# Spatial gating's rests: the last product of each half on 64 rows instead of 128, the two halves on different rows of TensorE

## The chip, the cores and the metric

The kernel runs on one core of one Trainium2 chip. The metric is the device time of one execution in microseconds, from three runs: their median is 718.81 us, the lowest 718.46, the highest 719.28. A profiled execution of the same kernel lies beside them.

## The reference, cut to what matters

Three layers in a row: a linear attention, a gated convolution layer, and a gated MLP whose second half is mixed over the tokens. The change is in the last one. With 8 batches, 576 tokens, width 512:

```
h = gelu(x @ w_in)                       # 1024 wide
u, v = h[..., :512], h[..., 512:]
v_n = (v - mean(v)) / sqrt(var(v) + 1e-6) * g_ln
v_s = einsum('ts,bsd->btd', w_sg, v_n) + b_sg[None, :, None]
out = x + (u * v_s) @ w_out
```

The line with `einsum` is the one that matters: for each batch a 576x576 matrix is multiplied with the 576x512 matrix of normalised `v`, so it sums over tokens.

## The kernel before, in words

Every large product is made with fp32r operands that are split in a high and a low part: `x*w` becomes `xh*wh + xl*wh + xh*wl`, three TensorE products that add into one PSUM bank. The 576 tokens of a batch are four tiles of 128 tokens and a rest of 64. The rests of several batches are handled together in other products.

The first 321 us do attention and the convolution layer; then comes a loop over the 8 batches that does the MLP. For each batch there are four values of `m` (128 columns of the width each). For one `m` TensorE makes `hu` (12 products of 512 columns), then `sg` for `c = 0` and `c = 1`, the two halves of 288 output tokens. After the four `m` come 48 products `hv` of the next batch and 48 products `out`, each of 512 columns.

One `sg` half (L685 to L697) is 14 products of 288 columns into one bank: three for each of the four token tiles (`v` high with weight high `sgw`, `v` low with `sgw`, `v` high with weight low `sgl`), and two for the 64 rests. The rests of two batches, one even and one odd, sit in the two halves of the 128 partitions. `Rests.hv` (L648) makes from them one operand for each batch, `r[i]`: its own 64 partitions hold the high part, the other 64 the low part. So the first rest product, with `sgw[:, NK]` (the 64 rest weights' high part, twice, one below the other), gives two of the three terms at once. The second rest product gives the third term, high part by low weights. It runs on all 128 rows too: its weight operand, one for even and one for odd batches, `sgw[:, NK + 1 + b % 2]`, holds the low weights in the one half and zeros in the other. `rest_weight` (L523) makes these once.

After the last product of a half VectorE scales the bank into `vs` (L697); after both halves `gated` (L699) multiplies with `u` on VectorE (L707), rounds to the high part on ScalarE (L708), and takes the low part on VectorE (L712), into `gg`, which sits in buffer `Z`. `wout2` (L717) reads it.

In the trace the names are those of reused buffers: `sg<-WV,X` is a rest product (`X` is `X32`, the rests' operand; `WV` holds `sgw`, `G` holds `sgl`, and `X0h`, `X0l`, `Q`, `K`, `V` hold the token tiles or the weights of `out`). The order on each engine is set by a scheduler that the tile framework runs at build time. There are 8 PSUM banks that take turns. The kernel's first part has one other place where TensorE is used in parts: `kv` (L337) makes for each head a 64x64 product, two heads in the two halves of the array's columns (forms `128*64` in the trace: 128 rows, 64 columns).

Of the kernel before, what the change touches and what calls it, by code (L numbers as in the profile page):

```python
# [10 lines left out]
F32R = mybir.dt.float32r  # L11
AF = mybir.ActivationFunctionType
ALU = mybir.AluOpType
# [6 lines left out]
P = 128  # L20
# [12 lines left out]
WC = 256  # L33

LINE = 128
ROOM = {"st": 128, "bst": 32, "bmv": 32, "gcol": 32, "gln": 32, "mhalf": 96, "eps": 32, "cw": 64, "T": S, "X32": 19 * 128}
APART = 8

ORDER = """
# [20 lines left out]
class Slots:  # L60
# [5 lines left out]
    def later(self, slots, fn, rank=1):  # L66

        self.waiting.append((self.now + slots, rank, fn))
# [14 lines left out]
def body(ctx, tc, qT, k, v, gcol, w_val, conv_w, w_out, w_in, g_ln, w_sgT, b_sg, w_out2, out, out_r):  # L83
# [8 lines left out]
    def sb(tag, shape, dtype=F32, bufs=1, o=0):  # L92
        count[0] += 1
        words = math.prod(shape)
        t = pool.tile([P, o + words], dtype, tag=tag, name=f"{tag}_{count[0]}", bufs=bufs,
                      padded_shape=[P, ROOM.get(tag) or -(-(o + words) // LINE) * LINE])[:, o:]
        if len(shape) == 1:
            return t
        d = [f"d{i}" for i in range(len(shape))]
        return t.rearrange(f"p ({' '.join(d)}) -> p {' '.join(d)}", **dict(zip(d, shape)))  # L100

    def tmp(n):

        return sb("T", [S], bufs=7)[:, :n]
# [11 lines left out]
    def f32(x):  # L116
        return x.bitcast(F32)
# [404 lines left out]

    def rest_weight():  # L523
        sgw = p2["sgw"]
        rwh, rwl = sgw[:, NK], [sgw[:, NK + 1], sgw[:, NK + 2]]
        raw = tmp(S)
        for i in range(2):
            dma(raw[i * DH:(i + 1) * DH], w_sgT[4 * P:, :])
        act(rwh, raw, AF.Copy)
        for i in range(2):  # L530
            a = slice(i * DH, (i + 1) * DH)
            z = slice((1 - i) * DH, (2 - i) * DH)
            tt(rwl[i][a], raw[a], f32(rwh[a]), op=ALU.subtract)
            tt(rwl[i][z], raw[z], raw[z], op=ALU.subtract)

    def sg_weight(stage):
        p2["sgw"] = sb("WV", [NK + 3, S], F32R)
        p2["sgl"] = sb("G", [NK, S], F32R)
        for t in range(NK):
            def parts(t=t):  # L540
                act(p2["sgw"][:, t], stage[:, t], AF.Copy)
                tt(p2["sgl"][:, t], stage[:, t], f32(p2["sgw"][:, t]), op=ALU.subtract)

            parts()
# [94 lines left out]
    class Rests:  # L639
# [6 lines left out]
            self.pr = pr  # L646

        def hv(self):  # L648
            r = [p2["r"][:, self.pr % 2, i] for i in range(2)]

            def parts(g):
                for i in range(2):
                    a = slice(i * DH, (i + 1) * DH)
                    o = slice((1 - i) * DH, (2 - i) * DH)
                    act(r[i][a], g[a], AF.Copy)
                    tt(r[i][o], g[a], f32(r[i][a]), op=ALU.subtract)

            hv(*self.y, parts)
            return r

    class Group:

# [19 lines left out]
            gemm3(ps, (p2["wiu"][:, 0], p2["wiu"][:, 1]), m, self.y[:, 0], self.y[:, 1])  # L682
            gelu2(ps, self.u[:, m])

    def sg(b, c, m, vt, rem, vs):  # L685
        ps = bank("sg", CH)
        sl = slice(c * CH, (c + 1) * CH)
        msl = slice(m * P, (m + 1) * P)
        sgw, sgl = p2["sgw"], p2["sgl"]
        mm = []  # L690
        for t in range(4):
            h, l = vt[t]
            mm += [(h, sgw[:, t, sl]), (l, sgw[:, t, sl]), (h, sgl[:, t, sl])]
        mm += [(rem, sgw[:, NK, sl]), (rem, sgw[:, NK + 1 + b % 2, sl])]
        for n, (a, w) in enumerate(mm):
            nc.tensor.matmul(ps, lhsT=a[:, msl], rhs=w, start=(n == 0), stop=(n == len(mm) - 1))  # L696
        later(0, lambda: stt(vs[:, sl], ps, gln_s[:, m:m + 1], p2["bsg"][:, sl], op0=ALU.mult, op1=ALU.add))  # L697

    def gated(b, m, vs, u, ur, gg, ggr):  # L699

# [196 lines left out]
    for b in range(1, B):  # L897
        moe = moes[b] if b == 1 else Moe(atts[b].xh, atts[b].xl, gate, y_main[b])
        nxt = atts[b + 1] if b + 1 < B else None
        nn = atts[b + 2] if b + 2 < B else None  # L900
        group = b % RG == RG - 1
        if b == 2:
            p2["wiv"], p2["wiu"] = (sb(n, [2, NK, D], F32R) for n in ("wiv", "wiu"))
            wi = split_weight(p2["wiv"], w_in, D, D) + split_weight(p2["wiu"], w_in, 0, D)
            behind(loaded, wi[0][0])
            behind(loaded, wi[1][0])
            wi_n = 0
        if b == 1:
            whole = unbroken(lambda: (nn.kv(0), nn.kv(1)))
        for s in range(4 if b == 1 else 0, 8):  # L910
            with tc.issue_after(whole) if whole else ExitStack():
                if s < 4:
                    moe.val(s)
                else:
                    moe.out(s - 4)
            whole = None
            if nxt and s < 3:
                nxt.o(s + 2)
            if nn and s == 3 and not group:
                whole = unbroken(lambda: (nn.kv(0), nn.kv(1)))  # L920
            if nn and s == 3:
                nn.load_q()
            if b + 3 < B and s == 5 and not group:
                atts.append(Attention(b + 3))
                atts[-1].load_kv()
            if nn and s in (6, 7) and not group:
                nn.o(s - 6)
            if nxt and s in ((4, 5) if b == 1 else (5, 7)):
                later(0, lambda a=nxt, m=2 * (s > 4) if b == 1 else s - 5: a.gates((m, m + 1)), 2)
            if s == 2:  # L930
                later(0, atts[b].rest_parts, 2)
            if (b, s) == (B - 3, 7):
                w2 = w2_pieces()
                wi += w2[:4]
            if s in {2: (1, 4, 7), 3: odd, 4: odd, 5: odd, 6: odd, 7: (0,)}.get(b, ()):
                later(0, lambda w=wi[wi_n][1], m=marks[-3]: behind(m, w), 3)
                if wi_n + 2 < len(wi):
                    later(0, wi[wi_n + 2][0], 4)
                wi_n += 1
            if b == B - 1:  # L940
                if s == 0:
                    v_alloc()
                if s == 4:
                    stage = sb("X32", [NK, S])
                    dma(stage, w_sgT[:4 * P, :].rearrange("(t p) s -> p t s", p=P))
                    toks = Tokens(0)
                    toks.load(0)
                if s > 4:
                    toks.load(s - 4)
                    later(0, lambda t=s - 5: toks.split(t), 1)  # L950
            tick()
            marks.append(latest())
        if group:
            moe = Moe(rest["x"][:, 0], rest["x"][:, 1], rest["g"], y_rest[b // RG])
            for s in range(8):
                with tc.issue_after(whole) if whole else ExitStack():
                    if s < 4:
                        moe.val(s)
                    else:
                        moe.out(s - 4)  # L960
                whole = None
                if nn and s == 1:
                    whole = unbroken(lambda: (nn.kv(0), nn.kv(1)))
                if b + 3 < B and s == 2:
                    atts.append(Attention(b + 3))
                    atts[-1].load_kv()
                if nn and s == 3:
                    nn.o(0)
                    nn.o(1)
                if b == B - 1:  # L970
                    if s == 0:
                        toks.split(3)
                    if s < 4:
                        toks.hv(s)
                    if s == 2:
                        rem = Rests(0)
                        later(1, rem.split, 1)
                    if s == 4:
                        sg_weight(stage)
                        rest_weight()  # L980
                        p2["r"] = sb("X32", [2, 2, D], F32R)
                    if s == 5:
                        y_r = Group.load(0)
                    if s == 6:
                        background(w2[4:], 2, 2)
                if b == B - 1 or s % 2:
                    tick()
# [6 lines left out]
    for b in range(B):  # L994
# [9 lines left out]
        for m in range(NK):  # L1004
            u = toks.hu(m)
            tick()
            vs = tmp(S)
            for c in range(2):
                sg(b, c, m, toks.v, rem[b % 2], vs)
                if c:  # L1010
                    gated(b, m, vs, u, grp.u, gg, ggr)
                tick()
            if more and m == 2:
                ntoks = Tokens(b + 1)
                ntoks.load(0)
                ntoks.load(1)
# [78 lines left out]
```

## Time and profile before

| what | value |
|---|---|
| median of 3 runs | 718.81 us (718.46 to 719.28) |
| the profiled execution's own time | 718.38 us |
| its span, first to last instruction | 716.6 us |
| TensorE (PE) busy | 708.3 us, 99% |
| VectorE (DVE) busy | 572.5 us, 80% |
| ScalarE (ACT) busy | 365.4 us, 51% |
| GpSimd (POOL) busy | 160.7 us, 22% |
| granted TensorE clock | full in all 40 slices |

Busy time is the union of an engine's instructions. A matmul's duration in the trace is longer than the step from its start to the next one's start, since matmuls overlap in the array; steps between starts are what adds up to the span. Start times are given in us from the span's start with two digits, durations in line views in ns.

### The profile page before, as it was taken

What the parts mean: (1) busy time and instruction counts of PE and PEld (TensorE: products, weight loads), DVE (VectorE), ACT (ScalarE), POOL (GpSimd) and SP (SyncE); (2) the same over time, 40 slices, a digit from 0 to 9 for tenths busy, and PEclk for the clock granted to TensorE, in tenths of its full rate; (3) what the DMA queues carried; (4) which work ended last, traced back from release to release, by engine and by line L of the source; (5) the groups of instructions that cost most, each with busy time, mean ns of one, the idle gap of its engine ahead of it and who ended that gap; (6) DMA issues with size and microseconds to landing.
All of it is one profiled execution on the core that took longest, in us unless ns stands there. A gap on an engine that the chain in (4) does not pass through costs nothing.

```text
span 716.6 us, 11759 instructions
## 1 busy us (share of the span) xinstructions
PE 708.3 (99%) x4462; PEld 619.6 (86%) x4462; DVE 572.5 (80%) x1111; ACT 365.4 (51%) x747; POOL 160.7 (22%) x180
## 2 busy tenths in 40 slices
PE   8999999999999999999999999999999999999998
PEld 8788888889888888899889888898899898898897
DVE  3999897999899999799867877857867767868662
ACT  2999966575666574664524434335334334335220
POOL 1558435434635532121000000100100100100000
PEclk9999999999999999999999999999999999999999
DMA  9994066227442113541231221122241122111302
GB/s 309 324 301 155 37 222 219 90 102 252 157 168 96 75 53 132 179 136 43 75 118 30 75 89 52 51 74 82 80 147 37 67 75 74 59 59 46 102 1 89
DMA packets 57241, 81.20 MB, mean 113 GB/s; under 512 B 3680, under 2 KB 30304, under 8 KB 56160
## 3 DMA queue, kind: packets, MB, share of 16 engines
q1 hardware_dynamic: 57184, 80.45, 33.5%
q8 instruction: 35, 0.57, 0.3%
q14 instruction: 22, 0.18, 0.1%
HBM read 61.56 MB, written 18.87 MB: 112 GB/s over the span
## 4 chain that ended last, share of the span: by engine, by line
PE 82%; DVE 12%; DMA 2%; ACT 1%; issue 1%; POOL 1%; SPq 0%; DVEq 0%; POOLq 0%
PE sg L696 17%; PE hv L587 14%; PE out L266 14%; PE hu L266 12%; PE y L266 11%; PE val L266 8%; DVE G L457 6%; PE o L358 2%; PE hur L266 2%; PE xT L394 1%; PE kv L337 1%; DVE st L368 1%; DMA V<-in_v_dram 1%; DMA wiu<-in_w_val_dram 1%; DVE T L387 1%
## 5 line engine op out<-in xcount | busy, mean ns | idle before, releaser
L457 DVE SCALAR_TENSOR_TENSOR G<-X,cw,G 128x576 f32<-128x576 f32 x128 | 99.0, 823 | 3.3 <-ACT G L454 3.2
L599 POOL TENSOR_TENSOR bmv<-bmv,mhalf 128x1 f32<-128x1 f32 x36 | 21.5, 597 | 342.4 <-DVE bmv L598 342.4
L266 PE MATMUL y<-Z,WOh 128*128 128x512 f32 (+1 forms) x320 | 96.0, 375 | 0.0
L587 PE MATMUL hv<-wiv,X1h 128*128 128x512 f32 x256 | 83.1, 390 | 0.0
L266 PE MATMUL out<-Z,K 128*128 128x512 f32 x256 | 83.0, 389 | 0.0
L266 PE MATMUL hu<-X1h,wiu 128*128 128x512 f32 x256 | 79.2, 391 | 0.0
L379 POOL TENSOR_TENSOR st<-st,mhalf 128x8 f32<-128x8 f32 x40 | 72.9, 1833 | 2.7
L266 PEld LDWEIGHTS y<-Z,WOh 128*128 128x128 f32 x320 | 57.9, 188 | 9.8
L576 ACT ACTIVATE T<-T 128x512 f32<-128x512 f32 x68 | 43.0, 633 | 44.2 <-DVE T L573 44.1
L266 PE MATMUL y<-Z,WOl 128*128 128x512 f32 (+1 forms) x160 | 57.9, 368 | 0.0
L266 PEld LDWEIGHTS out<-Z,K 128*128 128x128 f32 x256 | 48.1, 188 | 9.9
L587 PEld LDWEIGHTS hv<-wiv,X1h 128*128 128x128 f32 x256 | 47.7, 188 | 9.8 <-ACT X1h L564 0.3
L266 PEld LDWEIGHTS hu<-X1h,wiu 128*128 128x128 f32 x256 | 46.6, 188 | 8.3
L697 DVE SCALAR_TENSOR_TENSOR T<-sg,gln,WOl 128x288 f32<-128x288 f32 x64 | 32.8, 517 | 25.3 <-PE sg L696 25.2
L266 PE MATMUL hu<-X1l,wiu 128*128 128x512 f32 x128 | 50.0, 390 | 0.0
L587 PE MATMUL hv<-wiv,X1l 128*128 128x512 f32 x128 | 49.9, 390 | 0.0
L266 PE MATMUL out<-Z,V 128*128 128x512 f32 x128 | 49.8, 389 | 0.0
L708 ACT ACTIVATE Z<-T 128x512 fp32r<-128x512 f32 x32 | 20.3, 634 | 57.4 <-DVE T L707 57.3
L358 PEld LDWEIGHTS o<-kvbd,Q 128*128 128x128 f32 x320 | 39.9, 191 | 2.6 <-ACT kvbd L349 0.5
L358 PE MATMUL o<-kvbd,Q 128*128 128x128 f32 x320 | 40.7, 275 | 0.4 <-ACT kvbd L349 0.3
L266 PE MATMUL val<-X0h,WV 128*128 128x512 f32 x128 | 40.7, 399 | 0.0
L266 PE MATMUL val<-X1h,WV 128*128 128x512 f32 x128 | 40.3, 396 | 0.0
(180 smaller groups left out, 1712.7 us busy)
## 6 DMA issues: line engine op xcount, KB each, us to landing
y_main<-Y SPq DMA_DIRECT2D x8, 1024.0 KB, 4.2
raw<-y_main SPq DMA_DIRECT2D x32, 256.0 KB, 3.0
Y<-y_main SPq DMA_DIRECT2D x32, 256.0 KB, 3.8
out_dram<-Y SPq DMA_DIRECT2D x32, 256.0 KB, 2.3
Q<-in_qT_dram SPq DMA_DIRECT2D x7, 1152.0 KB, 5.5
K<-in_k_dram SPq DMA_DIRECT2D x7, 1024.0 KB, 5.9
V<-in_v_dram SPq DMA_DIRECT2D x7, 1024.0 KB, 9.2
raw<-in_w_in_dram SPq DMA_DIRECT2D x16, 256.0 KB, 5.1
```

Source lines behind the costliest of these rows:

```text
L266: nc.tensor.matmul(ps, lhsT=a[:, kt, msl], rhs=x[:, kt], start=(i == 0), stop=(i == 3 * NK - 1))
L337: nc.tensor.matmul(self.pk[j][h, h], lhsT=self.k[:, t, js][:, h], rhs=self.v[:, t, js][:, h], start=(t == 0), stop=(t == 4))
L358: nc.tensor.matmul(po[:, j * P:(j + 1) * P], lhsT=self.q[:, j, o:o + P], rhs=bd[:, j, :], start=True, stop=True)
L368: nc.vector.tensor_reduce(i["st"][:, 0], i["x3"], axis=AX.X, op=ALU.add)
L379: nc.gpsimd.tensor_tensor(st[:, 2], st[:, 1], mhalf, op=ALU.pow)
L457: stt(gate[:, m], x32[:, m, j:j + S], cw3[:, m, j:j + 1], gate[:, m], op0=ALU.mult, op1=ALU.add)
L576: act(w, w, AF.Tanh, scale=CG * AG)
L587: nc.tensor.matmul(ps, lhsT=a[:, kt], rhs=p2["wiv"][:, w, kt], start=(i == 0), stop=(i == 3 * NK - 1))
L599: nc.gpsimd.tensor_tensor(mv[:, 3:4], mv[:, 2:3], mhalf[:, 0:1], op=ALU.pow)
L696: nc.tensor.matmul(ps, lhsT=a[:, msl], rhs=w, start=(n == 0), stop=(n == len(mm) - 1))
L697: later(0, lambda: stt(vs[:, sl], ps, gln_s[:, m:m + 1], p2["bsg"][:, sl], op0=ALU.mult, op1=ALU.add))
L708: act(g[:, 0], x, AF.Copy)
```

## The change

Four edits.

1. `rest_weight` keeps one low-weight operand in place of two, with the low weights in both halves of the partitions and no zeros: one subtraction over 128 partitions in place of four instructions over 64.
2. `Rests.hv` makes a third operand `r[2]`, a copy of the high parts of both batches' rests, each in the other half of the partitions: two more ScalarE copies of 64x512 for every pair of batches.
3. `sg` leaves its bank open after 13 products.
4. A new `sg_last` closes both halves after that: two products of 64 rows, of which the one for `c = 0` uses the half of the rows that belongs to the batch (with `r[b % 2]`), and the one for `c = 1` the other half (with `r[2]`). VectorE's scaling of both halves comes after it.

```
-        tt(rwl[i][a], raw[a], f32(rwh[a]), op=ALU.subtract)     # for i in 0, 1
-        tt(rwl[i][z], raw[z], raw[z], op=ALU.subtract)
+    tt(rwl, raw, f32(rwh), op=ALU.subtract)
...
             act(r[i][a], g[a], AF.Copy)
+            act(r[2][o], g[a], AF.Copy)
             tt(r[i][o], g[a], f32(r[i][a]), op=ALU.subtract)
...
-        return r
+        return [(r[i], r[2]) for i in range(2)]
...
-    mm += [(rem, sgw[:, NK, sl]), (rem, sgw[:, NK + 1 + b % 2, sl])]
+    mm.append((rem[0], sgw[:, NK, sl]))
     for n, (a, w) in enumerate(mm):
-        nc.tensor.matmul(ps, lhsT=a[:, msl], rhs=w, start=(n == 0), stop=(n == len(mm) - 1))
-    later(0, lambda: stt(vs[:, sl], ps, ...))
+        nc.tensor.matmul(ps, lhsT=a[:, msl], rhs=w, start=(n == 0), stop=False)
+    return ps
+
+def sg_last(b, m, pss, rem, vs):
+    msl = slice(m * P, (m + 1) * P)
+    for c, ps in enumerate(pss):
+        sl = slice(c * CH, (c + 1) * CH)
+        i = (b + c) % 2
+        rows = slice(i * DH, (i + 1) * DH)
+        nc.tensor.matmul(ps, lhsT=rem[c][rows, msl], rhs=p2["sgw"][rows, NK + 1, sl], start=False, stop=True)
+        later(0, lambda sl=sl, ps=ps: stt(vs[:, sl], ps, gln_s[:, m:m + 1], p2["bsg"][:, sl], op0=ALU.mult, op1=ALU.add))
...
+        pss = []
         for c in range(2):
-            sg(b, c, m, toks.v, rem[b % 2], vs)
+            pss.append(sg(c, m, toks.v, rem[b % 2]))
             if c:
+                sg_last(b, m, pss, rem[b % 2], vs)
                 gated(b, m, vs, u, grp.u, gg, ggr)
```

The scheduler's order shows it. TensorE, second batch, `m = 1`, the end of the two halves. Before, where `sg_4103` is the bank of `c = 1` (and `sg_4085`, closed 14 products earlier, that of `c = 0`):

```order
L696 MATMUL sg_4103<-WV_3355,V_2700 128x288
L696 MATMUL sg_4103<-G_3356,K_2699 128x288
L696 MATMUL sg_4103<-WV_3355,X0h_3020 128x288 x2
L696 MATMUL sg_4103<-G_3356,X0h_3020 128x288
L696 MATMUL sg_4103<-WV_3355,X_455_3373 128x288 x2
L266 MATMUL hu_4119<-X1h_3756,wiu_1202 128x512 x2
```

After, where `sg_4084` is the bank of `c = 0` and `sg_4100` that of `c = 1` (the size in a row is that of the output, so the 64-row products, L702, read 128x288 as well):

```order
L693 MATMUL sg_4100<-G_3356,K_2699 128x288
L693 MATMUL sg_4100<-WV_3355,X0h_3020 128x288 x2
L693 MATMUL sg_4100<-G_3356,X0h_3020 128x288
L693 MATMUL sg_4100<-WV_3355,X_455_3370 128x288
L702 MATMUL sg_4084<-WV_3355,X_455_3370 128x288
L702 MATMUL sg_4100<-WV_3355,X_455_3370 128x288
L266 MATMUL hu_4118<-X1h_3755,wiu_1202 128x512 x2
```

The second rest product of `c = 0` has moved behind all of `c = 1`, and the two 64-row products stand side by side between 128-row ones. This holds for all 32 pairs of batch and `m`: 21 are followed by `hu`, 7 by `hv`, 3 by another `sg`, the last by `out`.

VectorE, last batch, `m = 3`, from the scaling of the halves on (`T_6964`, in after `T_6969`, is `vs`). Before:

```order
L573 SCALAR_TENSOR_TENSOR T_6955<-T_6955,hu_6942 128x512
L697 SCALAR_TENSOR_TENSOR T_6964<-sg_6965,gln_82,WOl_3458 128x288
L577 SCALAR_TENSOR_TENSOR T_6955<-T_6955,hu_6942 128x512
L697 SCALAR_TENSOR_TENSOR T_6964<-sg_6983,gln_82,WOl_3458 128x288
L707 TENSOR_TENSOR T_6964<-T_6964,T_6955 128x512
```

After:

```order
L569 SCALAR_TENSOR_TENSOR T_6960<-T_6960,hu_6947 128x512
L573 SCALAR_TENSOR_TENSOR T_6960<-T_6960,hu_6947 128x512
L703 SCALAR_TENSOR_TENSOR T_6969<-sg_6970,gln_82,WOl_3455 128x288
L703 SCALAR_TENSOR_TENSOR T_6969<-sg_6986,gln_82,WOl_3455 128x288
L713 TENSOR_TENSOR T_6969<-T_6969,T_6960 128x512
```

The scaling of `c = 0` has moved behind the second step of the gelu and stands right ahead of that of `c = 1`.

## Rows read from the trace of the kernel before

**Rows 1.** The page: span, busy time and share by engine, granted clock, chain

```profile
span 716.6 us, 11759 instructions
PE 708.3 (99%) x4462; PEld 619.6 (86%) x4462; DVE 572.5 (80%) x1111; ACT 365.4 (51%) x747; POOL 160.7 (22%) x180
...
PEclk9999999999999999999999999999999999999999
...
PE 82%; DVE 12%; DMA 2%; ACT 1%; issue 1%; POOL 1%; SPq 0%; DVEq 0%; POOLq 0%
```

**Rows 2.** Windows, MLP stage: length, busy us (count) PE PEld DVE ACT POOL, clock, DMA

```profile
321.00:697.00 376.00, 376.00 (x2077) 333.05 (x2076) 280.60 (x579) 147.59 (x274) 20.61 (x36) 1.00 0.22 70
```

**Rows 3.** Timeline of PE, end of both halves of one sg: start, us, line, operation, count

```profile
427.32 0.43 PE L696 MATMUL sg<-WV,X 128*128 128x288 f32 x2
427.58 0.43 PE L696 MATMUL sg<-WV,X0h 128*128 128x288 f32 x2
...
429.18 0.43 PE L696 MATMUL sg<-WV,X 128*128 128x288 f32 x2
429.45 0.63 PE L266 MATMUL hu<-X1h,wiu 128*128 128x512 f32 x2
```

**Rows 4.** Timeline of PE into two blocks of kv, and out of the second

```profile
188.81 0.39 PE L266 MATMUL val<-X0l,WV 128*128 128x512 f32 x1
189.03 0.61 PE L266 MATMUL val<-X0h,WV 128*128 128x512 f32 x2
189.49 0.39 PE L266 MATMUL val<-X0l,WV 128*128 128x512 f32 x1
189.81 0.28 PE L337 MATMUL kv<-V,K 128*64 128x64 f32 x2
...
162.38 2.55 PE L337 MATMUL kv<-V,K 128*64 128x64 f32 x80
164.86 0.61 PE L266 MATMUL val<-XR,WV 128*128 128x256 f32 x3
```

**Rows 5.** Line L337, a block's first two products, then later ones: count, ns min/median/max

```profile
L337 PE MATMUL kv<-V,K x2: 270/270/270, 189.8 to 189.8; 128*64 128x64 f32 x2
...
L337 PE MATMUL kv<-V,K x10: 222/222/222, 190.3 to 190.6; 128*64 128x64 f32 x10
```

**Rows 6.** Timeline of PE out of two blocks of kv, from a last kv product

```profile
47.71 0.22 PE L337 MATMUL kv<-V,K 128*64 128x64 f32 x1
47.86 0.73 PE L266 MATMUL val<-X0h,WV 128*128 128x512 f32 x2
48.43 0.40 PE L266 MATMUL val<-X0l,WV 128*128 128x512 f32 x1
48.66 0.62 PE L266 MATMUL val<-X0h,WV 128*128 128x512 f32 x2
...
14.18 0.28 PE L337 MATMUL kv<-V,K 128*64 128x64 f32 x3
14.39 0.94 PE L288 MATMUL o<-ident 128*128 128x128 f32 x6
```

**Rows 7.** Making the rests' operands, and their first uses: count, ns min/median/max, starts

```profile
L533 DVE TENSOR_TENSOR WV<-T,WV x2: 749/752/755, 312.6 to 313.3; 64x576 fp32r<-64x576 f32 x2
L655 ACT ACTIVATE X<-T x8: 621/630/634, 327.6 to 627.5; 64x512 fp32r<-64x512 f32 x8
...
L656 DVE TENSOR_TENSOR X<-T,X x2: 687/869/1051, 328.3 to 329.8; 64x512 fp32r<-64x512 f32 x2
L696 PE MATMUL sg<-WV,X x32: 291/294/300, 332.4 to 392.0; 128*128 128x288 f32 x32
```

**Rows 8.** Timeline behind the last sg: PE, DVE and ACT

```profile
696.75 0.39 PE L266 MATMUL out<-Z,K 128*128 128x512 f32 x1
...
696.95 0.52 DVE L697 SCALAR_TENSOR_TENSOR T<-sg,gln,WOl 128x288 f32<-128x288 f32 x1 [0.75 <-PE sg L696]
...
698.89 0.69 DVE L712 TENSOR_TENSOR Z<-T,Z 128x512 fp32r<-128x512 f32 x1 [0.56 <-ACT Z L708]
```

More of the change, by code (lines that the diff above doesn't have):

```diff
@@ L35 @@
 LINE = 128
-ROOM = {"st": 128, "bst": 32, "bmv": 32, "gcol": 32, "gln": 32, "mhalf": 96, "eps": 32, "cw": 64, "T": S, "X32": 19 * 128}
+ROOM = {"st": 128, "bst": 32, "bmv": 32, "gcol": 32, "gln": 32, "mhalf": 96, "eps": 32, "cw": 64, "T": S, "X32": 24 * 128}
 APART = 8
@@ L524, in rest_weight @@
         sgw = p2["sgw"]
-        rwh, rwl = sgw[:, NK], [sgw[:, NK + 1], sgw[:, NK + 2]]
+        rwh, rwl = sgw[:, NK], sgw[:, NK + 1]
         raw = tmp(S)
@@ L529, in rest_weight @@
         act(rwh, raw, AF.Copy)
-        for i in range(2):
-            a = slice(i * DH, (i + 1) * DH)
-            z = slice((1 - i) * DH, (2 - i) * DH)
-            tt(rwl[i][a], raw[a], f32(rwh[a]), op=ALU.subtract)
-            tt(rwl[i][z], raw[z], raw[z], op=ALU.subtract)
+        tt(rwl, raw, f32(rwh), op=ALU.subtract)
     def sg_weight(stage):
-        p2["sgw"] = sb("WV", [NK + 3, S], F32R)
+        p2["sgw"] = sb("WV", [NK + 2, S], F32R)
         p2["sgl"] = sb("G", [NK, S], F32R)
@@ L648, in hv @@
         def hv(self):
-            r = [p2["r"][:, self.pr % 2, i] for i in range(2)]
+            r = [p2["r"][:, self.pr % 2, i] for i in range(3)]
             def parts(g):
@@ L683, in hu, with sg @@
             gelu2(ps, self.u[:, m])
-    def sg(b, c, m, vt, rem, vs):
+    def sg(c, m, vt, rem):
         ps = bank("sg", CH)
@@ L693, in sg @@
             mm += [(h, sgw[:, t, sl]), (l, sgw[:, t, sl]), (h, sgl[:, t, sl])]
-        mm += [(rem, sgw[:, NK, sl]), (rem, sgw[:, NK + 1 + b % 2, sl])]
+        mm.append((rem[0], sgw[:, NK, sl]))
         for n, (a, w) in enumerate(mm):
-            nc.tensor.matmul(ps, lhsT=a[:, msl], rhs=w, start=(n == 0), stop=(n == len(mm) - 1))
-        later(0, lambda: stt(vs[:, sl], ps, gln_s[:, m:m + 1], p2["bsg"][:, sl], op0=ALU.mult, op1=ALU.add))
+            nc.tensor.matmul(ps, lhsT=a[:, msl], rhs=w, start=(n == 0), stop=False)
[8 more added lines that the diff above has]
+            later(0, lambda sl=sl, ps=ps: stt(vs[:, sl], ps, gln_s[:, m:m + 1], p2["bsg"][:, sl], op0=ALU.mult, op1=ALU.add))
     def gated(b, m, vs, u, ur, gg, ggr):
@@ L980, in body @@
                         rest_weight()
-                        p2["r"] = sb("X32", [2, 2, D], F32R)
+                        p2["r"] = sb("X32", [2, 3, D], F32R)
                     if s == 5:
```

## The prediction

> **What bounds the kernel now.** I read the page first: TensorE is busy for 708.3 of 716.6 us at a clock that is full in every slice, and the chain that ended last is 82% TensorE [rows 1]. Then the stretch that the change touches. Over the 376 us of the MLP stage TensorE has no idle time at all, VectorE is busy for 281 and ScalarE for 148 of it [rows 2]. So what counts in this stage is the length of TensorE's own queue; work on VectorE or ScalarE costs nothing as long as it doesn't make TensorE wait. TensorE's price is the step from one start to the next, not the duration of a row. In the timeline of one `sg` half, 14 products go from 427.58 to 429.45: 1.87/14 = 0.134 us each, and there is no break where `hu` follows [rows 3].
>
> **The change part by part.**
>
> *Products taken away.* For each of 32 pairs of batch and `m` two 128-row products, 2 x 0.134 = 0.267 us, give way to two 64-row ones. A product's step goes by its columns (0.134 us for 288, 0.23 for 512 [rows 3, 4]), which stay at 288, so I take a 64-row product by itself to be no shorter. The gain can only come from the two running at the same time. No row shows products on different rows together, but `kv` shows them on different columns: 80 products of 64 columns take 2.48 us from 162.38 to 164.86 [rows 4], and the two of a pair start together (both inside 0.28 us, each lasting 0.270) [rows 4, 5]. That is 2.48/40 = 0.062 us for a pair. I take the offset within a pair as 0.01 us (0.28 less 0.27). Side by side the pair costs 0.134 + 0.01, a gain of 0.124 us for each of 32: 4.0 us. Its bounds are 0 (one after the other) and 4.3 (no offset).
>
> *Going into 64-row use and coming out.* This is the term on which all hangs, and before has no row for it with rows, only with columns: `kv`, which also stands between full products. Three things can be read there.
> - Going in: `val` products of 512 columns start every 0.23 us (189.03 to 189.49 for two), but the first `kv` starts 0.32 us after the last `val` [rows 4]. That is 0.09 more than the step: a pause in which the array seems to empty first.
> - The first weights are not loaded behind a running product: the first two `kv` products last 270 ns, later ones 222 [rows 5], so 0.05 us for 64 columns of weights. Here the weights have 128 columns.
> - Coming out: the last `kv` starts at 47.71, the next full product at 47.86, 0.15 later, and the one after it another 0.34 later, since two products take from 47.86 to 48.43, 0.57, and 0.23 is the step [rows 6]. A pair of `kv` takes 0.05 to 0.06, so 0.15 holds 0.10 of emptying; and 0.57 - 2 x 0.23 = 0.11 is the exposed weight load of 128 columns, twice the 0.05 for 64. Nothing else explains it: at 14.39 the products that follow read only a constant that was ready at the start, and still the last `kv`, which ends at 14.46 and lasted 0.22, so began at 14.24, is followed after 0.15 [rows 6].
>
> Together 0.09 + 0.11 + 0.10 + 0.11 = 0.41 us for one excursion, with 0.11 for the first weights, as for a load of 128 columns (with the 64-column figure, 0.05, it would be 0.35). The order shows 32 excursions, each of one pair. 32 x 0.41 = 13.1 us. Bounds: 0, if the halves of the rows can be used without a change of mode, and 16.6, if also the two halves' weights load one after the other (0.11 more each). I take 13.1: `kv` is the only row of the kind, and its two sides, going in and coming out, agree.
> The Trainium skill says the same without a difference between rows and columns: in "TensorEngine Tiling (Array Packing)", section Key Properties, a change of the tiling mode, not just of the tile, drains TensorE. For columns the trace agrees (0.09 and 0.10 us); no run here shows it for rows. By that rule the sum below is the one that I make; without it, it would be the first rival's.
>
> *VectorE.* Each half's scaling now follows the pair, so `c = 0`'s comes some 14 products later. Its reader, `gated`, waited for `c = 1` anyway; only the 0.52 us of the `c = 0` scaling now stand between the last product and `gated`. In batches 0 to 6 the 48 `hv` products stand between that and most of `out`. At the end of the kernel `out` starts at 696.75 and the last part of `gg` is ready at 699.58 [rows 8]; the order puts 29 products of 0.23 us, 6.6 us, ahead of the first that reads it. 2.8 + 0.5 us fit in: 0. Without that cover it would be 0.5 us, once. Banks stay open some 2 us longer, of a turn of 8 banks and three per `m` of about 6.5 us: 0. `rest_weight` saves three operations of 0.75 us [rows 7] on VectorE, once, where TensorE doesn't wait: 0.
>
> *ScalarE.* Two more copies of 0.63 us for each of four pairs of batches [rows 7], 5 us in all on an engine with half its time free. They stand in front of the second half's low part, so they delay the operands by 1.26 us. For the first pair the last of them began at 329.8 and lasted up to 1.05, ready by 330.9, and the first use is at 332.4 [rows 7]: 1.5 us left, of which the scheduler's new order may use up more by putting rest products earlier. 0, with a bound of 2 us, once; SP's queue swaps one load of `Y` with one of `raw`, with no reader near: 0.
>
> *The sum.* 13.1 - 4.0 = +9.1 us. From the profiled execution's own 718.38 us that is 727.5. The median of the runs stands 0.43 higher, at 718.81, and a median is what will be compared: 727.9.
>
> **The rivals.**
> - *Rows are not columns: no emptying, and the pair runs together.* Then only the gain is left: 718.8 - 4.0 = 714.8, faster. For it: no row shows an excursion to half the rows being charged. Against it: `kv`, on all its sides. It decides the sign: as soon as one excursion costs more than 0.124 us, less than a third of `kv`'s 0.41, the change loses. The Trainium skill's "TensorE: Matmul & The Clock Gate", Part 3, has a result of this kind: small products on different row groups run together, their span is one product plus about 4 ns for each further tile. By it this change gains 4.1 us, 32 x (0.134 - 0.004). No run here shows it for rows, and it says nothing there of full products around the small ones.
> - *Half the price:* the emptying is paid but the weights load behind it (0.19 in place of 0.41), or the weights are paid and not the emptying (0.22). 32 x 0.19 - 4.0 = +2.1, 32 x 0.22 - 4.0 = +3.0: 720.9 to 721.8.
> - *The full price and no pair:* the two products run one after the other. +13.1: 731.9. Against it: the pairs of `kv`, and the order, which has nothing between the two products in any of 32 places.
> - *It does nothing:* the 64-row products run one after the other as full ones do, without a change of mode. 718.8.
>
> **How the numbers follow.** The full price with the pair 0.67, half the price 0.09, full price and no pair 0.05, the gain alone 0.13, nothing 0.06. Measurements of this kernel tell about 0.2% (1.4 us) from no change. Faster is the gain alone, 0.13; same is 0.06; slower the other three, 0.81. The range goes from 721.0, which takes in about the dearer half of the half-price cases, to 732.0, with the full price without a pair and the bound of the weights in part: about 0.78.
>
> **What would show it.** In the trace of after: TensorE's first 64-row product some 0.22 us after the last full one starts in place of 0.13; two 64-row products with starts 0.01 apart; 0.23 or so from them to the next full product; and that one's follower late by 0.11. The 32 places together hold the whole difference, and the stretch before 321 us is unchanged. I am wrong if the steps around the pair stay at 0.13 (the gain is then 4 us), or if TensorE shows idle time with a wait for VectorE or ScalarE in the MLP stage, above all at the first rest products near 330 us.

## The result, and the profile after

The changed kernel takes 726.85 us (median of 4, 726.74 to 727.01) against 718.74 us for the kernel before: a ratio of 1.0109 with a 95% interval of 1.0097 to 1.0121, so 1.1% slower, by 8.1 us where 9.1 were forecast. The profiled execution took 726.81 us, 8.4 above that of before.

The page of the changed kernel, its span, busy times, granted clock and chain, which answer to [rows 1]:

```profile
span 725.0 us, 11770 instructions
PE 716.1 (99%) x4462; PEld 618.2 (85%) x4462; DVE 572.0 (79%) x1108; ACT 369.8 (51%) x755; POOL 162.4 (22%) x180
...
PEclk9999999999999999999999999999999999999999
...
PE 86%; DVE 8%; DMA 3%; ACT 1%; issue 1%; SPq 1%; POOL 0%; DVEq 0%; POOLq 0%
```

TensorE has as many products as before and is busy 7.8 us longer; its weight loads, PEld, are busy slightly less. ScalarE has its 8 more copies. The clock is full in every slice.

A window over the MLP stage of the changed kernel, with the columns of [rows 2]:

```profile
329.00:705.20 376.20, 376.20 (x2029) 324.34 (x2027) 271.96 (x552) 146.14 (x270) 19.44 (x33) 1.00 0.21 67
```

There is no idle time on TensorE, as before: nothing waits for VectorE or ScalarE. But in 376 us it gets through 2029 products, where the kernel before gets through 2077. The time went into the steps. Hardly any of it lies ahead of this stage: the first `sg` product starts at 321.42 us in the trace of before and at 321.73 in that of after, so 8.1 of the 8.4 us between the two profiled executions come behind it.

The timeline of TensorE at the end of one pair of halves, the counterpart of [rows 3] (start, us, line, operation, form, count):

```profile
431.48 0.29 PE L693 MATMUL sg<-G,Q 128*128 128x288 f32 x1
431.62 0.29 PE L693 MATMUL sg<-WV,X 128*128 128x288 f32 x1
431.84 0.40 PE L702 MATMUL sg<-WV,X 64*128 64x288 f32 x2
432.17 0.73 PE L266 MATMUL hu<-X1h,wiu 128*128 128x512 f32 x2
432.73 0.39 PE L266 MATMUL hu<-X1l,wiu 128*128 128x512 f32 x1
```

Here the whole price can be read. Full products follow each other by 0.13 us; the pair of 64-row products starts 0.22 after the last of them. Both lie within 0.40 us, so they run together. `hu` starts 0.33 after them, and its first two products take 0.56 where two such steps are 0.46. From 431.62 to 432.73 that is 1.11 us. The kernel before takes three steps of 0.134 and two of 0.23 for the same work, with two full products in place of the pair: 0.86. 0.25 us, 32 times, is 8.0 us.

All 64 products of line L702 in the changed kernel (count, ns min/median/max, first and last start), and what its weight loads stood idle for:

```profile
L702 PEld LDWEIGHTS sg<-WV,X x64: 182/183/184, 330.3 to 704.8; 64*128 64x128 f32 x64
L702 PE MATMUL sg<-WV,X x64: 391/395/400, 330.3 to 704.8; 64*128 64x288 f32 x64
...
  issue: 5.2, 32
```

Every one of them lasts 391 to 400 ns, 0.10 more than the 294 of a full product of the same width [rows 7]. I read this as weights that are loaded in the open, with no product running meanwhile, in all 32 places; the run with fewer columns, below, tests it. The 32 idle times ahead of the weight loads, 5.2 us together, end with nothing that the profile shows; I take them for the array emptying, which no row shows directly.

### The profile page after: what moved, and what is told of

It is laid out like the page before. It is cut to its first block, busy times and chain, and to the rows that moved or that the text cites. A ratio compares the mean times of both kernels' runs of the same rounds, so it can differ in the third digit from the quotient of the medians.

```text
span 725.0 us, 11770 instructions
## 1 busy us (share of the span) xinstructions
PE 716.1 (99%) x4462; PEld 618.2 (85%) x4462; DVE 572.0 (79%) x1108; ACT 369.8 (51%) x755; POOL 162.4 (22%) x180
## 4 chain that ended last, share of the span: by engine, by line
PE 86%; DVE 8%; DMA 3%; ACT 1%; issue 1%; SPq 1%; POOL 0%; DVEq 0%; POOLq 0%
PE sg L693 15%; PE hv L583 14%; PE out L266 14%; PE hu L266 13%; PE y L266 11%; PE val L266 10%; DVE G L457 4%; DMA V<-in_v_dram 3%; PE o L358 3%; PE kv L337 2%; PE xT L394 2%; PE hur L266 2%; PE sg L702 1%; DVE st L368 1%; DVE T L387 1%
## 5 line engine op out<-in xcount | busy, mean ns | idle before, releaser
L266 PE MATMUL hu<-X1h,wiu 128*128 128x512 f32 x256 | 81.5, 399 | 0.0
L703 DVE SCALAR_TENSOR_TENSOR T<-sg,gln,WOl 128x288 f32<-128x288 f32 x64 | 30.1, 512 | 23.0 <-PE sg L702 22.7
L568 ACT ACTIVATE T<-hv 128x512 f32<-128x512 f32 x36 | 21.4, 594 | 43.6 <-PE hv L583 43.6
```

The lines of the kernel that those rows point to most:

```text
L266: nc.tensor.matmul(ps, lhsT=a[:, kt, msl], rhs=x[:, kt], start=(i == 0), stop=(i == 3 * NK - 1))
L568: act(w, ps, AF.Square)
L703: later(0, lambda sl=sl, ps=ps: stt(vs[:, sl], ps, gln_s[:, m:m + 1], p2["bsg"][:, sl], op0=ALU.mult, op1=ALU.add))
```

## The experiments

The theory: TensorE changes its mode where 64-row products stand between 128-row ones, and each such excursion, the way into 64-row use and out of it, costs 0.39 us beyond its products (0.09 until the array is empty, 0.105 for weights loaded in the open, and the same two again on the way out), while a pair side by side saves 0.128 (a step of 0.132 less the 0.004 between the two starts). The rivals: the new order, the later closing of `c = 0` or ScalarE's copies; a price for each 64-row product or for rows left idle; a pair that gains nothing.

### The new order and the copies alone

```
-            rows = slice(i * DH, (i + 1) * DH)
-            nc.tensor.matmul(ps, lhsT=rem[c][rows, msl], rhs=p2["sgw"][rows, NK + 1, sl], start=False, stop=True)
+            nc.tensor.matmul(ps, lhsT=rem[c][:, msl], rhs=p2["sgw"][:, NK + 1 + i, sl], start=False, stop=True)
```

(and `rest_weight` as in the kernel before)

> The changed kernel's order and its extra ScalarE copies, but the last rest products of both halves on all 128 rows, with the zero-padded weights of the kernel before. No 64-row product is left. Theory (the price is that of going into 64-row use and out of it): the time of the kernel before, 718.7 us within 0.7, and steps of 0.13 us through the whole end of sg. Rival (the later closing of c = 0, the copies on ScalarE or the new order cost the time): it stays near 726.9 us.

718.24 us, ratio to before 1.0001 (0.999 to 1.0012). The timeline of TensorE at the same place:

```profile
429.03 0.29 PE L697 MATMUL sg<-WV,X 128*128 128x288 f32 x1
429.16 0.42 PE L705 MATMUL sg<-WV,X 128*128 128x288 f32 x2
429.42 0.62 PE L266 MATMUL hu<-X1h,wiu 128*128 128x512 f32 x2
429.88 0.39 PE L266 MATMUL hu<-X1l,wiu 128*128 128x512 f32 x1
```

The two closing products stand where the pair stood, and every step is regular: 0.13, 0.26 for two, 0.46 for two of `hu`. So the order, the later closing, and the copies cost nothing that can be measured, and the 8 us belong to the use of 64 rows.

### Both products of a pair on the same rows

```
-            i = (b + c) % 2
+            i = b % 2
...
-            nc.tensor.matmul(ps, lhsT=rem[c][rows, msl], ...)
+            nc.tensor.matmul(ps, lhsT=rem[0][rows, msl], ...)
```

> The changed kernel, but both 64-row products of a pair use the same 64 rows, those of the batch, so they can't run side by side; the 32 excursions stay. Theory (a pair side by side costs one product, an excursion 0.39 us beyond its products): the second product of a pair starts 0.13 us after the first in place of 0.004, so 32 x 0.128 = 4.1 us more than the changed kernel, 730.9 us, the step out unchanged near 0.32 us. If the second product's weights can't be loaded while the first runs on the same rows, 0.105 us more each, 734.3 us. Rival (the pair gains nothing anyway): 726.9 us.

730.84 us, ratio 1.0171 (1.0158 to 1.0184): 12.1 us over before. TensorE's timeline, and that of its weight loads:

```profile
339.37 0.29 PE L693 MATMUL sg<-WV,X 128*128 128x288 f32 x1
339.59 0.53 PE L702 MATMUL sg<-WV,X 64*128 64x288 f32 x2
340.05 0.73 PE L266 MATMUL hu<-X1h,wiu 128*128 128x512 f32 x2
...
339.59 0.30 PEld L702 LDWEIGHTS sg<-WV,X 64*128 64x128 f32 x2 [0.16 <-issue]
```

The two now take 0.53 us in place of 0.40, one product's step more. So in the change the two do run side by side, and this is worth 4.0 us (730.84 less 726.85), as forecast. The second product's weights don't cost a second 0.105: both loads are over within 0.30 us of the first product's start, while the first product's row lasts 0.395, so the second load runs during the first product, although on the same rows. (The two products here have the same weights, loaded twice; in the next run they differ, and the step is the same.) One thing of the expectation was off. The second product starts not 0.13 but 0.24 us after the first. The 0.105 more is the open load, which stands inside the first product's row: it lasts 395 ns, the second's 291. The way out is then 0.22 and not 0.32; the sum is the same.

### Two m in one excursion

```
+            if m % 2 == 0:
+                held = []
             for c in range(2):
                 pss.append(sg(c, m, toks.v, rem[b % 2]))
                 if c:
-                    sg_last(b, m, pss, rem[b % 2], vs)
-                    gated(b, m, vs, u, grp.u, gg, ggr)
+                    held.append((m, pss, vs, u))
+                    if m % 2:
+                        for m_, pss_, vs_, u_ in held:
+                            sg_last(b, m_, pss_, rem[b % 2], vs_)
+                        for m_, pss_, vs_, u_ in held:
+                            gated(b, m_, vs_, u_, grp.u, gg, ggr)
```

> The changed kernel, but the last products of two neighbouring m are made together: 16 excursions of four 64-row products in place of 32 of two. Theory (0.39 us for an excursion whatever it holds, a gain of 0.128 us for each pair): against the kernel before 16 x 0.39 - 32 x 0.128 = +2.1 us, 720.8 us, with a step of 0.13 us from one pair to the next inside an excursion. Rival (each pair or each 64-row product has its own price): it stays near 726.9 us. A second rival (four open banks and the later scaling make TensorE wait): idle time of TensorE, over 721.5 us.

720.81 us, 2.1 over before; ratio 1.0034 (1.0023 to 1.0045). (The profiled execution took 723.35 us: its granted clock was lower in one slice some 18 to 36 us from the start, far ahead of this stretch.) TensorE's timeline:

```profile
432.19 0.29 PE L693 MATMUL sg<-WV,X 128*128 128x288 f32 x1
432.40 0.53 PE L702 MATMUL sg<-WV,X 64*128 64x288 f32 x4
432.86 0.74 PE L266 MATMUL hu<-X1h,wiu 128*128 128x512 f32 x2
433.44 0.39 PE L266 MATMUL hu<-X1l,wiu 128*128 128x512 f32 x1
```

Four 64-row products take 0.46 us from 432.40 to `hu`, where two take 0.33: a second pair costs one step, with its weights loaded while the first runs. The steps in (0.21 in these rounded starts, 0.22 as the median of the 16 places) and behind (0.58 for two) are those of the changed kernel to 0.02 us. So the price is the excursion's, for two products and for four.

### Each half closed in its own place

```
-                if c:
-                    sg_last(b, m, pss, rem[b % 2], vs)
+                sg_last(b, m, pss, rem[b % 2], vs, c)      # only half c
+                if c:
```

> Each half closes with its own 64-row product at its end, as the kernel before closes it: 64 excursions of one product, no pair. Theory: 64 x 0.39 = 25.0 us over the kernel before, 743.7 us; each 64-row product takes a step of 0.22 us in and 0.32 us out, and the full product behind it 0.105 us more than its own step. Rival (the price belongs to two products that close two banks at once): less than 10 us over the kernel before.

743.33 us, ratio 1.0343 (1.0325 to 1.036): 24.6 us over before, 0.385 for each of 64 excursions of one product. TensorE's timeline where the second half follows the first:

```profile
704.31 0.29 PE L693 MATMUL sg<-WV,X 128*128 128x288 f32 x1
704.53 0.39 PE L702 MATMUL sg<-WV,X 64*128 64x288 f32 x1
704.86 0.53 PE L693 MATMUL sg<-WV,X0h 128*128 128x288 f32 x2
705.23 0.29 PE L693 MATMUL sg<-G,X0h 128*128 128x288 f32 x1
```

0.22 in, 0.33 out, and 0.37 for two products whose steps are 0.26 together. One product alone pays what a pair pays.

### Fewer rows without 64

```
-            nc.tensor.matmul(ps, lhsT=rem[c][:, msl], rhs=p2["sgw"][:, NK + 1 + i, sl], start=False, stop=True)
+            rows = slice(0, 96 if i == 0 else P)
+            nc.tensor.matmul(ps, lhsT=rem[c][rows, msl], rhs=p2["sgw"][rows, NK + 1 + i, sl], start=False, stop=True)
```

(against the kernel of the first experiment)

> As e1_order_only, but 32 of the 64 last products use 96 rows in place of 128 (the 32 rows left out have zero weights). Theory (the price is for the change of mode, which 64 rows bring and 96 do not, not for rows left idle): 718.3 us within 0.7, all steps near 0.13 us. Rival (any product on fewer than 128 rows pays): 16 or more excursions at 0.39 us, 724.5 us or more.

718.72 us, ratio 0.9999 (0.999 to 1.0008). The closing products by form (count, busy us, mean ns, idle before), and TensorE's timeline at one of 96 rows:

```profile
L706 PE MATMUL sg<-WV,X 96*128 96x288 f32 x32 | 9.5, 298 | 0.0
...
L706 PE MATMUL sg<-WV,X 128*128 128x288 f32 x32 | 9.3, 296 | 0.0
...
332.64 0.30 PE L706 MATMUL sg<-WV,X 96*128 96x288 f32 x1
332.77 0.43 PE L697 MATMUL sg<-WV,X 128*128 128x288 f32 x2
```

A product on 96 rows lasts as long as one on 128, and the next full one starts 0.13 us after it; in all 32 places the steps into it and out of it are 0.13 to 0.14. So it brings no pause, and it isn't rows left idle that cost.

### Fewer columns of weights

```
-            nc.tensor.matmul(ps, lhsT=rem[c][rows, msl], ..., start=False, stop=True)
+            nc.tensor.matmul(ps[:96], lhsT=rem[c][rows, msl][:, :96], ..., start=False, stop=True, skip_group_check=True)
```

(and `sg` marks its 13th product as its bank's last)

> The changed kernel, but the 64-row products load 96 columns of weights in place of 128 and make 96 of the 128 output rows; the other 32 rows of each half lack the rests' third term. Theory (the first weights of an excursion are loaded in the open, 0.105 us for 128 columns, and the emptying does not depend on them): the step from the pair to the next full product falls by a quarter of 0.105, from 0.325 to 0.299 us, the step in stays at 0.22, the follower's lateness at 0.105; 32 x 0.026 = 0.8 us less than the changed kernel, 726.0 us. Rival (what lies between is one fixed pause): no step moves, 726.9 us.

726.46 us, ratio to before 1.0111 (1.0087 to 1.0136). In the time the expected 0.8 us against the changed kernel can't be told from none; the steps tell it. The line with its weight loads, and TensorE's timeline:

```profile
L702 PEld LDWEIGHTS sg<-WV,X x64: 156/156/157, 330.6 to 704.7; 64*96 64x96 f32 x64
L702 PE MATMUL sg<-WV,X x64: 367/368/373, 330.6 to 704.7; 64*96 64x288 f32 x64
...
691.13 0.29 PE L693 MATMUL sg<-WV,X 128*128 128x288 f32 x1
691.35 0.38 PE L702 MATMUL sg<-WV,X 64*96 64x288 f32 x2
691.66 0.73 PE L266 MATMUL hu<-X1h,wiu 128*128 128x512 f32 x2
692.22 0.39 PE L266 MATMUL hu<-X1l,wiu 128*128 128x512 f32 x1
```

A 64-row product lasts 368 ns in place of 395, and the way out is 0.31 in place of 0.33 (0.30 is the median of the 32 places, from their starts). The weight load itself is shorter by the same 27 ns, 156 against 183. 27 ns for a quarter of the columns is 0.108 us for 128: the open weight load. The way in, 0.22, and the lateness behind, 0.10, don't move. So the pause is two things, a load that goes with the columns of weights, and a rest that doesn't, which I take for the emptying.

### All four m in one excursion

This could have beaten both kernels, by 1 us, if nothing waited. The edit is that of two `m`, with the four `hu` ahead, all eight banks held until `m = 3`, and 8 temporary buffers in place of 7.

```
+        us = []
+        for m in range(NK):
+            us.append(toks.hu(m))
+            tick()
...
+                    if m == NK - 1:
...
-        return sb("T", [S], bufs=7)[:, :n]
+        return sb("T", [S], bufs=8)[:, :n]
```

> As e3_two_m, but all four m of a batch are closed together: 8 excursions of eight 64-row products, with one more temporary buffer, the four hu products ahead of the sg ones, and all 8 banks open at once. Theory alone: against the kernel before 8 x 0.39 - 32 x 0.128 = -1.0 us, 717.7 us, since more than three pairs pay for an excursion. Rival (with all banks taken hv has to wait behind each excursion for VectorE to scale the first bank): idle time of TensorE at 7 places, 0.2 to 0.6 us each, 1.4 to 4.2 us, so 719 to 722 us.

730.87 us, ratio 1.0157 (1.0137 to 1.0177). TensorE's waits in the whole kernel (who, for whom: us in total, times, longest), and its timeline at one excursion:

```profile
PE hv L583 <- DVE T L703: 4.5, 7, 2.2
PE out L266 <- ACT Z L714: 4.5, 1, 4.5
...
394.72 0.29 PE L693 MATMUL sg<-WV,X 128*128 128x288 f32 x1
394.94 0.79 PE L702 MATMUL sg<-WV,X 64*128 64x288 f32 x8
396.03 0.47 PE L583 MATMUL hv<-wiv,X1h 128*128 128x512 f32 x1 [0.31 <-DVE T L703]
396.34 0.39 PE L583 MATMUL hv<-wiv,X1l 128*128 128x512 f32 x1
```

Four windows of it, with the columns of [rows 2] (the granted clock is the third number from the end):

```profile
347.00:349.00 2.00, 2.00 (x5) 1.63 (x6) 2.00 (x6) 0.00 (x0) 0.00 (x0) 0.50 0.45 131
350.00:352.00 2.00, 2.00 (x10) 1.65 (x9) 2.00 (x7) 0.64 (x2) 0.00 (x0) 1.00 0.00 0
708.00:710.00 2.00, 2.00 (x6) 1.53 (x5) 2.00 (x7) 0.51 (x2) 0.00 (x0) 0.50 0.00 0
712.00:714.00 2.00, 2.00 (x11) 1.65 (x10) 0.00 (x0) 0.00 (x0) 0.00 (x0) 1.00 0.04 8
```

The eight products are as cheap as forecast, 0.79 us with the loads. But `hv` waits at all 7 places for VectorE to scale a bank, 4.5 us, and at the end of the kernel `out` waits 4.5 us for `gg`, which I had not counted: with all the scaling left to the end, the first product behind the excursion needs `gg`, and the cover of 29 products that the prediction names is gone. So the rival holds, and costs more than I gave it. The two longest of these waits, 2.2 us at 345 and 4.5 us at 702, cost a second time: while TensorE stood idle in them its granted clock fell to half, the lower of its two levels, and stayed there until about 350 and 712 us. By the steps of the same products at the full clock, that is some 1.5 and 2.5 us more (an estimate from the starts in this trace). The theory's -1.0, 9.0 of waits and 4 of clock make the 12 us over before.

## Why the prediction was right

**The bound.** That only TensorE's own queue counts in this stage held: no idle time in the window after, and the copies and the order alone cost nothing (1.0001).

**Products taken away.** The pair was taken from columns, where `kv` showed it, over to rows. It holds: 4.0 us between products on different rows and on the same rows, 4.0 forecast. Their starts are 3 to 5 ns apart in all 32 places of the trace, where I had put 10.

**Going in and out.** This was the term on which all hung, taken from `kv`'s 64 columns for want of a row with 64 rows: 0.41 us forecast. The runs give 0.385 (64 excursions of one product), 0.379 (12.1 us for 32 without a pair), and 0.39 (2.1 + 4.1 us for 16 of two pairs). The parts were right too. The way in was 0.09 over the step, as forecast. The lateness behind was 0.10 to 0.11. The open weights were put at 0.11, twice `kv`'s 0.05 for twice the columns, and are 0.10 to 0.11, shown by the run with 96 columns. Most of what the forecast of 9.1 us has over the measured 8.1 comes from this term, 0.025 us too high, 0.8 us for 32: I read starts to 0.01 us from single places and rounded each of the four parts up; the emptying on the way out, above all, was taken with 0.05 for a pair of `kv`, and with the 0.062 that the prediction itself works out it would have been 0.09 in place of 0.10. With the emptying alike at both ends (0.09 in and out) and 0.105 for a load, the four make 0.39. That rows would cost what columns cost was an assumption, for which the trace of before had no row; the runs bear it out. Two multiplications in the prediction are slightly off, without any weight in its sum: 32 x (0.134 - 0.004) is 4.2 and not 4.1, and 29 x 0.23 is 6.7 and not 6.6.

The section Key Properties of "TensorEngine Tiling (Array Packing)" in the Trainium skill says that a change of the tiling mode drains TensorE. For rows, which the kernel before could not show, the trace after agrees: 0.09 us more than a step on the way in. The larger half of the price here, 0.21 of 0.39 us, is the two open weight loads.

**The rivals.** The gain alone needed an excursion under 0.124 us; it costs three times that. It was the right thing to weigh, since the pair alone does gain what it says. Half the price is excluded by the four steps, each found in full. Full price and no pair is the run on the same rows, 730.84 us where I had 731.9. That nothing changes is excluded by the 8.1 us.

**The covers at nothing.** VectorE's later scaling at the end of the kernel was put at 0, with 29 products as its cover. That held for the change (no wait of `out` in the window after or behind it), and the run with four `m` shows what it costs without that cover: 4.5 us of waiting. ScalarE's copies ahead of the first rest products caused no wait.

## What to carry to other kernels

Half a contraction saved by packing two products on the halves of the rows is worth one product's step for each pair, and costs a fixed price for each time that TensorE leaves its full mode, here three times as much. So count the excursions, not the products. By these two prices at least four pairs of 288 columns are needed in one excursion (0.39 against 0.128 each) before it pays, and the banks held open for this must not make anything wait; no run here met both, and none with 64-row products was faster than the kernel before. Look in a trace for a block of half-size products that is already there, cut by rows or by columns: here the edges of `kv`, cut by columns, showed the price for rows to within 0.03 us of 0.39 (the extra step in, the longer first products, and the late second product behind it).

## What the runs showed of the hardware that I had not expected

Two 64-row products on the same rows one after the other don't pay a second open weight load: the second's weights come in while the first runs (0.53 us for both, 0.13 more than for a pair side by side). And a product on 96 rows has neither the pause (steps of 0.13 us around it) nor the open load (298 ns against 296), so the price begins somewhere between 96 and 64 rows, with no run in between, and not with rows left out as such.
